# Linear attention and a mixture of experts: each row of x carries its gate as a fifth piece of 128 words

## The chip, the cores and the metric

The kernel runs on one core of a Trainium2 chip. The metric is the device time of one execution in microseconds; lower is better. The engines have separate, in-order instruction streams and meet by semaphores: TensorE (PE in the profile, with its weight loads as PEld), VectorE (DVE), ScalarE (ACT), GpSimd (POOL) and SyncE (SP), which here only issues DMAs.

## What is computed

Two stages, the second on the result of the first:

```python
# attention, per batch b and head h: q, k, v (8, 8, 576, 64), w_phi (64, 128)
proj = x @ w_phi;  proj -= max(abs(proj), -1)
phi(x) = concat([exp(proj), exp(-proj)], -1)
attn = (phi(q) @ (phi(k).T @ v)) / (phi(q) @ sum_s phi(k) + 1e-6)
x = attn.transpose(0, 2, 1, 3).reshape(4608, 512)
# experts: w_gate (512, 8), w1 (8, 512, 1024), w2 (8, 1024, 512)
logits = x @ w_gate
expert = argmax(logits);  gate = softmax(logits)[expert]
out[t] = gate[t] * (relu(x[t] @ w1[expert[t]]) @ w2[expert[t]])
```

Every row goes through one expert only.

## The kernel before, in words

**Attention.** 16 units (4 groups of 4 pairs of heads) are worked off one after another, up to about 385 us. SP loads `xr` (q and k, line 235) and `vt` (v, lines 345 and 358). A hand-written plan (`PLAN_...`, `plan_of`) says at which step of a unit which load, split and product is issued; an entry "C" calls `constants2()` in unit 2. The finished rows of x go to `x_dram` in HBM by `store_rows` (lines 217 and 222), a table of 4608 rows of 512 words. The routing of a group works out each row's expert and gate; `gate_store` writes the gate (four equal words a row) by the same helper to a second table, `g_dram`, of 4608 x 4 words.

**Blocks.** The rows of one expert are put together into blocks of 128. Two blocks of an expert make a pair. There are 19 pairs (u = 0 to 18, blocks 0 to 37) and then single blocks (u = 19, 20, 21: blocks 38, 39, 40; more lie in a conditional part, which is not taken here). `gidx` holds for each block the numbers of its rows in x, `sidx` those in the output. Blocks 0 to 2, the lead, are put together from the first three groups while the last one is still in attention.

**Fetching a block.** GpSimd gathers rows by indirect DMA (`fetch_rows`, line 861), in one of two ways:

- `gather_rows`: one DMA, 128 rows of 512 words, into the tile `xg`. Used for u < 4 and for the single blocks. `x_parts` then turns the block with four TensorE transposes against `ident` (line 1104).
- `gather_quarters`: four DMAs of 128 rows of 128 words. The indices `qidx` are such that partition p gets quarter rows of 32-row groups, so that one VectorE instruction that turns 32 x 32 squares (line 1099) turns the whole block. Used where `by_quarters(u)` holds: 4 <= u < 19.

Either way ScalarE casts the turned block `px` into a high part `xh` (line 1105), and VectorE takes the rest `xl` (line 1106). All products of float32 numbers are made of such high and low parts, three matmuls each. `xg` has four buffers, so a gather waits until the block four places earlier has been turned.

**Gates.** `gather_gates` fetches a block's 128 gates from `g_dram` by one more indirect DMA into a tile `gate` (six buffers), issued by `gates(u)` beside `gather(u + 1)`.

**Expert stage.** For a pair, `pair_first` makes `pm` (lines 1123 to 1125), ScalarE makes `hh` (line 1130) and VectorE `hl` (line 1131), and `pair_second` adds up `po` (lines 1143 to 1145), a quarter of the 1024 hidden words at a time; `first_product`, `h_parts` and `second_product` do the same for a single block. `write` scales `po` by the gate on ScalarE into `ob` (line 1191, three buffers) and sends it out by an indirect DMA (line 1193), which waits for the write before it. SP loads the weights `raw`, ScalarE casts them to `wh` (line 1057), VectorE, and GpSimd for a few, take the rest `wl` (line 1058).

The order of instructions on each engine is worked out by the framework's scheduler from the program (`behind(a, b)` makes it put a after b); GpSimd's and SP's DMAs each use eight semaphores in turn (DMASW and DMAHW in the rows below).

## Time and profile before

| | before |
|---|---|
| median of 3 runs | 885.82 us (885.74 to 887.44) |
| the profiled execution | 887.59 us, span 885.9 us |
| granted TensorE clock, mean | 0.991 |
| indirect gathers of row quarters (x120) | 153.4 us, 1279 ns each |
| indirect gathers of gates (x41) | 50.3 us, 1228 ns each |
| indirect gathers of whole rows (x11) | 11.4 us, 1036 ns each |
| indirect writes of the output (x41) | 47.7 us, 1163 ns each |
| VectorE turns (x30) | 33.0 us, 1102 ns each |
| TensorE transposes of x (x44) | 7.5 us, 288 ns each |

A row of a timeline has the start in us, the duration, the engine, the line of the kernel, the operation, the tile written and those read, and in brackets how long the engine stood idle before it and what released it ("issue": nothing that the profile shows). Groups give the count, the busy time and the mean in ns. Consecutive instructions of one kind are put together as xN. A matmul's end is modelled and overlaps the next, so that TensorE's pace is the distance of starts.

### The profile page before, as it was taken

How to read it: one execution, taken by the hardware profiler on the slowest of the kernel's cores; microseconds unless marked ns; L12 is line 12 of the kernel's file. 1: busy time of each engine (PE TensorE's matmuls, PEld its weight loads, DVE VectorE, ACT ScalarE, POOL GpSimd, SP SyncE). 2: the span in 40 equal slices, each digit the busy share in tenths (PEclk: the TensorE clock that was granted, in tenths of full speed). 3: DMA queues.
4: the chain of work that ended last, by engine and by line, in shares of the span. 5: the costliest groups of instructions: out<-in, count | busy, mean ns of one | idle time of the engine just before them, and what ended most of it. 6: DMA issues, size and time to landing. Idle time of an engine off the chain costs nothing. (4 is left out here: it accounts for less than half of the span.)

```text
span 885.9 us, 18042 instructions
## 1 busy us (share of the span) xinstructions
PE 866.7 (98%) x6617; PEld 812.4 (92%) x6617; DVE 620.0 (70%) x1041; ACT 571.7 (65%) x874; POOL 547.1 (62%) x398
## 2 busy tenths in 40 slices
PE   9999999999999999999899999999999999999996
PEld 6999999999999999998688999998999989999884
DVE  6678878878887788759487666666766667765441
ACT  5888888888888888553465555555555555555662
POOL 5677667776676668553667888746876466312331
PEclk9999999999999999999899999999999999999998
DMA  6233334333343333351253154531545544445540
GB/s 203 84 98 98 107 112 95 82 95 104 111 113 110 111 111 71 108 185 20 82 162 112 55 171 125 173 110 49 160 126 164 184 160 142 135 142 188 200 141 15
DMA packets 69548, 106.65 MB, mean 120 GB/s; under 512 B 13582, under 2 KB 31502, under 8 KB 69456
## 3 DMA queue, kind: packets, MB, share of 16 engines
q1 hardware_dynamic: 59312, 84.50, 31.8%
q0 software_dynamic: 9472, 20.81, 7.6%
q8 instruction: 53, 0.87, 0.4%
q14 instruction: 39, 0.32, 0.1%
q10 hardware_dynamic: 672, 0.15, 0.1%
HBM read 128.42 MB, written 20.26 MB: 168 GB/s over the span
## 5 line engine op out<-in xcount | busy, mean ns | idle before, releaser
L1058 DVE TENSOR_TENSOR wl<-raw,wh 128x1024 fp32r<-128x1024 f32 x160 | 196.1, 1235 | 111.6 <-ACT wh L1057 79.7
L1057 ACT CAST wh<-raw 128x1024 fp32r<-128x1024 f32 x168 | 174.9, 1048 | 94.9 <-PE po L1145 41.5
L861 POOL DMA_INDIRECT xg<-x_dram,qidx x120 | 153.4, 1279 | 76.2 <-DVE px L1099 37.1
L448 PE MATMUL pn<-kf,qp 128*128 128x73 f32 (+1 forms) x1152 | 185.5, 256 | 0.0
L313 POOL TENSOR_TENSOR kl<-e,kh 128x1024 fp32r<-128x1024 f32 x45 | 107.5, 2388 | 106.7 <-ACT kh L311 99.1
L448 PEld LDWEIGHTS pn<-kf,qp 128*128 128x128 f32 x1152 | 172.5, 190 | 0.5
L1125 PE MATMUL pm<-xh,wl 128*128 128x256 f32 x608 | 172.4, 284 | 0.5 <-issue 0.5
L1124 PE MATMUL pm<-xl,wh 128*128 128x256 f32 x608 | 172.6, 284 | 0.1
L1123 PE MATMUL pm<-xh,wh 128*128 128x256 f32 x608 | 171.9, 283 | 0.0
L285 DVE TENSOR_REDUCE mx<-ps_proj 128x4 f32<-128x512 f32 (+1 forms) x160 | 101.0, 633 | 59.6 <-PE ps_proj L281 56.9
L1143 PE MATMUL po<-wh,hh 128*128 128x512 f32 x304 | 120.8, 398 | 3.9 <-issue 3.9
L1144 PE MATMUL po<-wl,hh 128*128 128x512 f32 x304 | 120.2, 395 | 0.6 <-issue 0.6
L1124 PEld LDWEIGHTS pm<-xl,wh 128*128 128x128 f32 x608 | 116.6, 192 | 3.7 <-issue 0.8
L1123 PEld LDWEIGHTS pm<-xh,wh 128*128 128x128 f32 x608 | 116.7, 192 | 2.9
L1145 PE MATMUL po<-wh,hl 128*128 128x512 f32 x304 | 119.2, 393 | 0.0
L1125 PEld LDWEIGHTS pm<-xh,wl 128*128 128x128 f32 x608 | 116.5, 192 | 0.8 <-issue 0.7
L286 DVE TENSOR_TENSOR t<-ps_proj,mx 128x512 f32<-128x512 f32 (+1 forms) x160 | 101.4, 635 | 4.9
L378 PE MATMUL pk<-kh,vl 128*64 128x256 f32 x300 | 101.6, 339 | 0.0
L378 PE MATMUL pk<-kh,vh 128*65 128x256 f32 x300 | 99.5, 332 | 1.5 <-ACT kvT L410 1.5
L378 PE MATMUL pk<-kl,vh 128*65 128x256 f32 x300 | 100.3, 334 | 0.0
L245 POOL TENSOR_TENSOR xl<-xr,xh 128x640 fp32r<-128x640 f32 (+1 forms) x60 | 96.8, 1633 | 2.1 <-ACT xh L244 2.1
L1130 ACT ACTIVATE hh<-pm 128x512 fp32r<-128x512 f32 x76 | 45.4, 597 | 76.4 <-PE pm L1125 56.4
(217 smaller groups left out, 1902.9 us busy)
## 6 DMA issues: line engine op xcount, KB each, us to landing
raw<-w SPq DMA_DIRECT2D x168, 512.0 KB
vt<-vv SPq DMA_DIRECT2D x15, 640.0 KB
x_dram<-xrow SPq DMA_DIRECT2D x30, 256.0 KB
xr<-kT SPq DMA_DIRECT2D x15, 320.0 KB
xr<-qT SPq DMA_DIRECT2D x15, 320.0 KB
xr<-kT SPq DMA_DIRECT2D x17, 256.0 KB
xr<-qT SPq DMA_DIRECT2D x17, 256.0 KB
xg<-x_dram,qidx POOLq DMA_INDIRECT x120
```

The costliest lines, as they stand in the source:

```text
L313: eng.tensor_tensor(kl, e[:, 0:m], kh, op=ALU.subtract)
L378: return T.matmul(st["pk", bb][0:n, hh, :], (vl if j == 1 else vh)[:, 2 * (c + (bb if c == 8 else 0)) + hh, 0:n], (kl if j == 2 else kh)[: ...
L448: m = T.matmul(pn[:, i - a, :] if c < 8 else pn[:, 2 + hh : 6 : 2, :], qp[:, s, s0 + hh, :], st["kf"][:, hh, s, c // 4, :] if c < 8 else s ...
L861: return G.indirect_dma_start(out=out, out_offset=None, in_=source[0:rows], in_offset=bass.IndirectOffsetOnAxis(ap=index, axis=0), bounds_ ...
L1057: A.copy(th, raw[k])
L1058: m = (G if k in (POOL_LO0 if u == 0 else POOL_LO if u >= NPAIR else ()) else V).tensor_tensor(tl, raw[k], th, op=ALU.subtract)
L1123: T.matmul(pm[:, i], th, xh[:, k, :], start=(k == 0), stop=False)
L1124: T.matmul(pm[:, i], th, xl[:, k, :], start=False, stop=False)
L1125: T.matmul(pm[:, i], tl, xh[:, k, :], start=False, stop=(k == KD - 1))
L1143: T.matmul(po, hh[:, i, r], th[:, c], start=(i == j == 0), stop=False)
L1144: T.matmul(po, hh[:, i, r], tl[:, c], start=False, stop=False)
L1145: T.matmul(po, hl[:, i, r], th[:, c], start=False, stop=(i == 1 and j == 3))
```

## The change

1. `x_dram` gets rows of 640 words: 512 of x, four with the gate (columns 512 to 515, written by `store_rows` as before to `g_dram`), and 124 zeros. The zeros come from a new tile `nought` (one GpSimd memset in `constants2`) and are written by four SP DMAs of 128 x 9 x 124 words, one for each group, in units 2 to 5 of the plan's "C".
2. `g_dram`, `gather_gates`, `gates` and their 41 DMAs are gone. `xg` has five pieces of 128 words. A gather of whole rows brings the gate with it; `gather_quarters` fetches a fifth piece, whose indices (a fifth column of `qidx`, one more VectorE operation) are those of the rows in their plain order. `x_parts` ends with a VectorE copy of one word per row, `gate <- xg[:, 4, 0:1]`.
3. `by_quarters(u)` holds for all u >= 4: the single blocks too come in pieces and are turned by VectorE. Row gathers go from 11 to 8, pieces from 120 to 165, VectorE turns from 30 to 33, TensorE transposes of x from 44 to 32.
4. `spread` and the two halves of `eg` use buffers of the pool `op`.

```diff
-    x_dram = dram.tile([NT, DM], F32, name="x_dram")
-    g_dram = dram.tile([NT, XW], F32, name="g_dram")
+    x_dram = dram.tile([NT, XQ * P], F32, name="x_dram")
...
             elif what == "C":
                 if st["u"] == 2:
                     constants2()
+                if 2 <= st["u"] < 2 + NG:
+                    g = st["u"] - 2
+                    rows = x_dram[g * NC * P : (g + 1) * NC * P, DM + XW :]
+                    nc.sync.dma_start(
+                        rows.rearrange("(c p) w -> p c w", p=P), nought.unsqueeze(1).to_broadcast([P, NC, P - XW])
+                    )
...
-            store_rows(g, gt, g_dram, 0, XW, c0, n)
+            store_rows(g, gt, x_dram, DM, XW, c0, n)
...
-        xg = xgp.tile([P, 4, P], F32, name="xg")
-        quarters = x_dram.rearrange("t (q d) -> (t q) d", q=4)
-        for c in range(4):
-            behind(fetch_rows(xg[:, c, :], quarters, qidx[:, c, b : b + 1], 4 * NT), st["experts"])
+        xg = xgp.tile([P, XQ, P], F32, name="xg")
+        for c in range(XQ):
+            behind(fetch_rows(xg[:, c, :], parts_dram, qidx[:, c, b : b + 1], XQ * NT), st["experts"])
         return xg
 
-    def gather_gates(b, after):
-        gate = xgp.tile([P, XW], F32, name="gate", bufs=6)
-        index, rows = (gidx0, NEARLY * P) if b < NLEAD else (gidx, NT)
-        behind(fetch_rows(gate, g_dram, index[:, b : b + 1], rows), after)
-        return gate
+    parts_dram = x_dram.rearrange("t (q d) -> (t q) d", q=XQ)
...
-        spread = raw2.tile([P, 4, P], F32, name="spread")
+        spread = op.tile([P, 4, P], F32, name="spread", tag="ob", bufs=3)
...
-        V.tensor_scalar(qidx, pq, 4.0, quad, op0=ALU.mult, op1=ALU.add)
+        V.tensor_scalar(qidx[:, 0:4], pq, float(XQ), quad, op0=ALU.mult, op1=ALU.add)
+        V.tensor_scalar(qidx[:, 4], st["rows"], float(XQ), 4.0, op0=ALU.mult, op1=ALU.add)
...
     def by_quarters(u):
-        return 4 <= u < NPAIR
+        return u >= 4
...
-            V.transpose(px, xg.rearrange("p c (d k) -> p c k d", k=KD))
+            V.transpose(px, xg[:, 0:4].rearrange("p c (d k) -> p c k d", k=KD))
...
         V.tensor_tensor(xl, px, xh, op=ALU.subtract)
+        gate = xgp.tile([P, 1], F32, name="gate", bufs=6)
+        V.tensor_copy(gate, xg[:, 4, 0:1])
+        st["gate", blocks(u)[i]] = gate
```

In the order of the instructions, the change shows at these three places. (Rows give the line, the operation, the tiles with their numbers and the semaphores that the instruction waits for; the change's lines are a few higher or lower than those of before.)

VectorE, at the end of pair u = 1 and in pair u = 2 (the profile's 456 to 467 us). Before, behind the last `hl` of u = 1:

```order
L1131 SCALAR_TENSOR_TENSOR hl_6699<-pm_6673,hh_6698 128x512 [waits Activation_49]
L1058 TENSOR_TENSOR wl_6944<-raw6_5828,wh_6943 128x1024 [waits DMAHW5_49,PE_49,Activation_49]
L1058 TENSOR_TENSOR wl_6872<-raw0_5816,wh_6871 128x1024 [waits DMAHW2_49,PE_49,Activation_49]
L1131 SCALAR_TENSOR_TENSOR hl_6794<-pm_6768,hh_6793 128x512 [waits Activation_49]
L1058 TENSOR_TENSOR wl_6939<-raw1_5818,wh_6938 128x1024 [waits DMAHW4_49,Activation_49]
L1058 TENSOR_TENSOR wl_7039<-raw7_5830,wh_7038 128x1024 [waits DMAHW7_49,Activation_49]
```

And now (`xg_6719` and `xg_6735` are blocks 8 and 9, which pair u = 4 will use):

```order
L1133 SCALAR_TENSOR_TENSOR hl_6694<-pm_6668,hh_6693 128x512 [waits Activation_49]
L1107 COPY gate_7126<-xg_6719 128x1 [waits DMASW0_49,Activation_49]
L1107 COPY gate_7192<-xg_6735 128x1 [waits DMASW5_49,Activation_49]
L1063 TENSOR_TENSOR wl_6941<-raw6_5833,wh_6940 128x1024 [waits DMAHW1_49,PE_49,Activation_49]
L1063 TENSOR_TENSOR wl_6867<-raw0_5821,wh_6866 128x1024 [waits DMAHW6_49,PE_49,Activation_49]
L1133 SCALAR_TENSOR_TENSOR hl_6787<-pm_6761,hh_6786 128x512 [waits Activation_49]
```

Two copies stand between that `hl` and the next weight splits. They wait for the fifth pieces of blocks 8 and 9 (DMASW0, DMASW5) and for ScalarE to be done with the `gate` buffers.

GpSimd, at the same place. Before, the second block's pieces, the two writes with the next gates, and the next pieces:

```order
L861 DMA xg_6737<-x_dram_155,qidx_71 128x128 [waits DMASW3_49]
L1193 DMA out<-ob_6714,sidx0_74 4608x512 [waits DMASW4_49,Activation_49]
L861 DMA gate_7025<-g_dram_156,gidx_68 128x4 [waits DMASW5_49]
L861 DMA gate_7029<-g_dram_156,gidx_68 128x4 [waits DMASW6_49,Activation_49]
L1193 DMA out<-ob_6719,sidx_69 4608x512 [waits DMASW7_49,DMASW4_49]
L861 DMA xg_6999<-x_dram_155,qidx_71 128x128 [waits DMASW0_49,PE_49]
L861 DMA xg_6999<-x_dram_155,qidx_71 128x128 [waits DMASW1_49]
```

And now:

```order
L870 DMA xg_6735<-x_dram_156,qidx_71 128x128 [waits DMASW4_49]
L870 DMA xg_6735<-x_dram_156,qidx_71 128x128 [waits DMASW5_49]
L1195 DMA out<-ob_6709,sidx0_74 4608x512 [waits DMASW6_49,Activation_49]
L1195 DMA out<-ob_6714,sidx_69 4608x512 [waits DMASW7_49,DMASW6_49,Activation_49]
L870 DMA xg_6996<-x_dram_156,qidx_71 128x128 [waits DMASW0_49,DVE_49,PE_49]
L870 DMA xg_6996<-x_dram_156,qidx_71 128x128 [waits DMASW1_49]
```

The two gates between the writes are gone, and the fifth piece of block 9 stands ahead of the first write. The second write waits for the first (DMASW6) as it did before (DMASW4).

SP, in the early attention units. Before:

```order
L235 DMA xr_516<-kT 128x640 [waits DMAHW4_49,DMAHW0_49,Pool_49]
L235 DMA xr_575<-qT 128x640 [waits DMAHW5_49,Pool_49]
L235 DMA xr_638<-kT 128x512 [waits DMAHW7_49,Pool_49]
L345 DMA vt_697<-vv 128x1280 [waits DMAHW6_49,DMAHW3_49]
L235 DMA xr_719<-qT 128x512 [waits DMAHW0_49,Pool_49]
```

And now:

```order
L238 DMA xr_516<-kT 128x640 [waits DMAHW4_49,DMAHW0_49,Pool_49]
L238 DMA xr_575<-qT 128x640 [waits DMAHW5_49,Pool_49]
L598 DMA x_dram_156<-nought_147 128x9x124
L598 DMA x_dram_156<-nought_147 128x9x124 [waits DMAHW3_49]
L598 DMA x_dram_156<-nought_147 128x9x124 x2
L238 DMA xr_638<-kT 128x512 [waits DMAHW7_49,DMAHW6_49,Pool_49]
L348 DMA vt_697<-vv 128x1280
L238 DMA xr_719<-qT 128x512 [waits DMAHW0_49,Pool_49]
```

The four stores of zeros, which the program issues in four units, stand together between a load of q and the next load of k.

More of the change, by code (lines that the diff above doesn't have):

```diff
@@ L49 @@
 XW = 4
+XQ = 5
 Q = P // 4
@@ L81, in tile_linear_attention_moe @@
     eidx = keep.tile([1, NB], I32, name="eidx")
-    qidx = keep.tile([P, 4, NB], I32, name="qidx")
+    qidx = keep.tile([P, XQ, NB], I32, name="qidx")
     nblk = keep.tile([1, 1], I32, name="nblk")
@@ L139, in constants @@
         nc.scalar.dma_start(fold[0:D, :, D + 1 : W], w_gate.rearrange("(h d) e -> d h e", d=D))
+    nought = const.tile([P, P - XW], F32, name="nought")
     def constants2():
+        G.memset(nought, 0.0)
         G.memset(ltri, 1.0)
@@ L877, in gather_quarters @@
     def gather_quarters(b):
-        xg = xgp.tile([P, 4, P], F32, name="xg")
-        quarters = x_dram.rearrange("t (q d) -> (t q) d", q=4)
-        for c in range(4):
-            behind(fetch_rows(xg[:, c, :], quarters, qidx[:, c, b : b + 1], 4 * NT), st["experts"])
-        return xg
-    def gather_gates(b, after):
-        gate = xgp.tile([P, XW], F32, name="gate", bufs=6)
-        index, rows = (gidx0, NEARLY * P) if b < NLEAD else (gidx, NT)
-        behind(fetch_rows(gate, g_dram, index[:, b : b + 1], rows), after)
-        return gate
+        xg = xgp.tile([P, XQ, P], F32, name="xg")
+        for c in range(XQ):
+            behind(fetch_rows(xg[:, c, :], parts_dram, qidx[:, c, b : b + 1], XQ * NT), st["experts"])
+        return xg
+    parts_dram = x_dram.rearrange("t (q d) -> (t q) d", q=XQ)
     v_tiles = []
@@ L1008, in experts_of @@
         V.tensor_reduce(nblk, ends[:, 1], axis=AX.X, op=ALU.max)
-        eg = sg.tile([1, 2, NB, E], F32, name="eg")
+        eg = [op.tile([1, NB, E], F32, name="eg", tag="h") for _ in range(2)]
         places = ((first[0:1], ends[:, 0], 0, 2 * NPAIR), (start[0:1], ends[:, 1], 2 * NPAIR, NB))
@@ L1013, in experts_of @@
                 m = V.tensor_tensor(
-                    eg[:, j, n0:n1],
+                    eg[j][:, n0:n1],
                     iota_p[0:1, n0:n1].unsqueeze(2).to_broadcast([1, n1 - n0, E]),
@@ L1019, in experts_of @@
                 behind(m, st["places"])
-        G.tensor_tensor(eg[:, 0], eg[:, 0], eg[:, 1], op=ALU.subtract)
-        st["experts"] = G.tensor_tensor(eg[:, 0], eg[:, 0], iota_e[0:1].unsqueeze(1).to_broadcast([1, NB, E]), op=ALU.mult)
+        G.tensor_tensor(eg[0], eg[0], eg[1], op=ALU.subtract)
+        st["experts"] = G.tensor_tensor(eg[0], eg[0], iota_e[0:1].unsqueeze(1).to_broadcast([1, NB, E]), op=ALU.mult)
         with nc.allow_low_precision("experts are integers"):
-            V.tensor_reduce(eidx, eg[:, 0], axis=AX.X, op=ALU.add)
+            V.tensor_reduce(eidx, eg[0], axis=AX.X, op=ALU.add)
     st = {}
@@ L1080, in gather @@
                     st["xg", b] = gather_rows(gidx[:, b : b + 1], NT, st.get("experts"))
-    def gates(u):
-        if u < lim[0]:
-            for b in blocks(u):
-                if ("gate", b) not in st:
-                    st["gate", b] = gather_gates(b, st["experts"])
     def x_parts(u, i):
@@ L1219, in tile_linear_attention_moe @@
     go(nums[-8:])
-    st["low"] = weights(0, 3)
-    for b in range(NLEAD):
-        st["gate", b] = gather_gates(b, st["low"])
+    weights(0, 3)
     run(r1[1:3])
@@ L1252, in tile_linear_attention_moe @@
     quarters_of()
-    gates(1)
     gather(2)
@@ L1277, in tile_linear_attention_moe @@
                 gather(u + 2)
-                gates(u + 1)
             for du, k in AHEAD_W[j]:
@@ L1293, in step @@
     def step(u):
-        gates(u)
         gather(u + 3)
```

## The prediction

> **What bounds the kernel now.** I read the busy times first, then a table of windows, then the list of what each engine waited for, and last the timelines at the places that the change touches. From the page:
>
> ```profile
> span 885.9 us, 18042 instructions
> PE 866.7 (98%) x6617; PEld 812.4 (92%) x6617; DVE 620.0 (70%) x1041; ACT 571.7 (65%) x874; POOL 547.1 (62%) x398
> ```
>
> TensorE is busy for 866.7 of 885.9 us, so 19.2 us are idle. The windows (length, busy time of each engine with its instructions, granted clock, DMA share, GB/s) say where:
>
> ```profile
> 0.00:22.00 22.00, 20.17 (x94) 15.01 (x95) 15.29 (x35) 12.71 (x25) 11.56 (x41) 1.00 0.66 204
> 420.00:440.00 20.00, 15.64 (x82) 13.19 (x82) 7.42 (x13) 7.72 (x11) 13.89 (x13) 0.83 0.32 94
> 440.00:520.00 80.00, 79.86 (x514) 72.60 (x514) 58.90 (x62) 48.31 (x61) 58.70 (x46) 1.00 0.37 113
> 780.00:860.00 80.00, 79.96 (x475) 71.04 (x474) 41.88 (x44) 45.60 (x59) 22.39 (x15) 1.00 0.52 172
> 860.00:886.00 26.00, 17.51 (x85) 14.08 (x83) 4.82 (x6) 6.44 (x10) 5.97 (x4) 0.89 0.09 33
> ```
>
> In the expert part TensorE has no gap (79.86 of 80, 79.96 of 80). There a matmul that goes saves its own length, and a wait on VectorE or GpSimd costs only what it makes TensorE wait. The gaps are at the two ends and at 420 to 440, where 4.4 us are lost (20 - 15.64) and the clock is 0.83. That last gap is one wait; first TensorE's matmul behind it, then the ScalarE activation that it needed:
>
> ```profile
> 434.05 0.79 PE L1143 MATMUL po<-wh,hh 128*128 128x512 f32 x1 [3.90 <-issue]
> 433.39 0.60 ACT L1130 ACTIVATE hh<-pm 128x512 fp32r<-128x512 f32 x1 [6.05 <-remote]
> ```
>
> The activation stood 6.05 us after its matmuls could be done, and its releaser ("remote") is nothing that the profile shows.
>
> **The change, part by part.**
>
> 1. TensorE loses 12 transposes. The three single blocks (u = 19, 20, 21) are now turned by VectorE, so three groups of four go. Their rows, with the next instruction on TensorE:
>
> ```profile
> 828.94 0.65 PE L1104 MATMUL px<-ident,xg 128*128 128x128 f32 x4
> 829.35 0.48 PE L1143 MATMUL po<-wh,hh 128*128 128x512 f32 x1
> 845.97 0.63 PE L1104 MATMUL px<-ident,xg 128*128 128x128 f32 x4
> 846.44 0.82 PE L1170 MATMUL pht<-ident,h 128*128 128x128 f32 x6
> 847.30 0.19 PEld L1157 LDWEIGHTS pm<-wh,xh 128*128 128x128 f32 x1 [0.27 <-ACT xh L1105]
> 853.11 0.64 PE L1104 MATMUL px<-ident,xg 128*128 128x128 f32 x4
> 853.51 0.48 PE L1183 MATMUL po<-wh,hh 128*128 128x512 f32 x1
> ```
>
> The groups take 829.35 - 828.94 = 0.41, 0.47 and 0.40 us of TensorE's time, 1.28 in all. The matmul after two of them is drawn out, 0.48 instead of the usual 0.39 to 0.40, about 0.08 each. The second group is followed by a wait of 0.27 for the cast of its own result, which goes too, since that block is now turned a pair earlier. Sum 1.28 + 0.16 + 0.27 = 1.7; I take **-1.6** (from -1.3, the groups alone, to -1.7). TensorE stands behind no other engine there, so nothing else is late next.
>
> 2. GpSimd and VectorE in the pairs. The groups, with busy us and mean ns:
>
> ```profile
> L861 POOL DMA_INDIRECT xg<-x_dram,qidx x120 | 153.4, 1279 | 76.2 <-DVE px L1099 37.1
> L861 POOL DMA_INDIRECT gate<-g_dram,gidx x41 | 50.3, 1228 | 12.3 <-issue 11.7 <-ACT wh L1057 0.3 <-ACT xh L1105 0.3
> L628 DVE TENSOR_SCALAR spare<-spare 128x1 f32<-128x1 f32 x1 | 0.1, 147 | 0.0
> ```
>
> 41 gate gathers go. 33 blocks (30 of pairs, 3 single) now take five pieces: 165 instead of 120, and three row gathers go. That is 45 - 41 - 3 = +1 instruction: GpSimd's load is the same, twelve DMAs in a pair (8 + 2 + 2 before, 10 + 2 now), at 1.3 + 0.3 us each some 19 of the 22.5 us that a pair takes (from TensorE's row at 490.62, below, to the same row of the next pair at 513.10). What differs is the order. A gate used to come after the eight pieces and the write; now the fifth piece stands ahead of the write, and the output of a pair is sent later. VectorE gains three turns of 1.1 us (482.06, below), under pairs in which it is idle a quarter of the time, and 41 copies of one word per row. No row shows such a copy; it lies between nothing and the 1.1 us of a turn, and I take the 0.15 us of the operation on one word per row (L628): 41 x 0.15 = 6 us beside 620, hidden under TensorE at either end (41 x 1.1 = 45 of the 266 us in which VectorE is idle).
>
> The copies' price is where they stand. VectorE runs in order, and the order shows the copies of two blocks ahead of two splits (wl) and of the hl that TensorE needs. First for blocks 8 and 9:
>
> ```profile
> 446.57 1.94 POOL L861 DMA_INDIRECT xg<-x_dram,qidx  x1 [0.30 <-issue]
> 456.81 1.00 POOL L861 DMA_INDIRECT xg<-x_dram,qidx  x1 [0.30 <-issue]
> 446.41 4.62 DVE L1058 TENSOR_TENSOR wl<-raw,wh 128x1024 fp32r<-128x1024 f32 x4
> 459.75 1.23 DVE L1058 TENSOR_TENSOR wl<-raw,wh 128x1024 fp32r<-128x1024 f32 x1 [3.08 <-ACT wh L1057]
> 462.36 0.68 DVE L1131 SCALAR_TENSOR_TENSOR hl<-pm,hh 128x512 fp32r<-128x512 f32 x1
> 467.35 0.40 PE L1145 MATMUL po<-wh,hl 128*128 128x512 f32 x1
> 418.63 1.04 POOL L861 DMA_INDIRECT xg<-x_dram,gidx  x1 [5.97 <-DVE emp L980]
> 422.10 0.75 PE L1104 MATMUL px<-ident,xg 128*128 128x128 f32 x4 [0.46 <-DMA xg<-x_dram,gidx]
> ```
>
> Before, the eighth piece ended at 457.81. Two more at 1.0 + 0.3 (VectorE has no split there) end at 460.4. A gather lands 422.10 - 419.67 = 2.4 us after GpSimd's end, so the copies pass at 462.8, and hl, which ended 459.75 -> 463.04 = 3.3 us after the first split began, ends at 466.1. TensorE reads it at 467.35: stall **0**. With two drawn-out pieces (2 x 2.24) and the slowest landing that I find (6.6, below) the copies pass at 468.9 and hl ends at 472.2: stall 4.9.
>
> The Trainium skill ("GPSIMD Engine Reference", section "Key points") says that GpSimd shares its SBUF interfaces with VectorE and is held up by VectorE instructions with two SBUF inputs. The trace agrees: a piece takes 1.94 us beside the four wl splits at 446.41 and 1.00 when VectorE stands. By that rule the pieces can't be drawn out while VectorE waits for them, which leaves only the landing for the upper end.
>
> Second, blocks 10 and 11, whose pieces stand behind block 3's write, and that behind block 2's:
>
> ```profile
> 458.38 1.02 POOL L1193 DMA_INDIRECT out<-ob,sidx  x1 [0.57 <-ACT ob L1191]
> 465.98 1.02 POOL L1193 DMA_INDIRECT out<-ob,sidx  x1 [3.92 <-DMA out<-ob,sidx]
> 478.31 1.42 POOL L861 DMA_INDIRECT xg<-x_dram,qidx  x1 [0.31 <-issue]
> 482.06 1.13 DVE L1099 STREAM_TRANSPOSE px<-xg 128x512 f32<-128x512 f32 x1
> 483.57 1.23 DVE L1058 TENSOR_TENSOR wl<-raw,wh 128x1024 fp32r<-128x1024 f32 x1 [0.38 <-ACT wh L1057]
> 486.13 0.68 DVE L1131 SCALAR_TENSOR_TENSOR hl<-pm,hh 128x512 fp32r<-128x512 f32 x1
> 490.62 0.39 PE L1145 MATMUL po<-wh,hl 128*128 128x512 f32 x1
> 513.10 0.39 PE L1145 MATMUL po<-wh,hl 128*128 128x512 f32 x1
> ```
>
> A write held the next one until 465.98 - 459.40 = 6.6 us after its own end. Block 2's write now ends at 461.7, block 3's starts at 468.3, and ten pieces from 469.6 at 1.28 + 0.30 end at 485.4. They land at 487.7 (before: 479.73 to 482.06, 2.3 us). hl began 486.13 - 483.57 = 2.56 us after the first split and takes 0.68, so it ends at 491.0 against 490.62: stall **0.4**. With all pieces at 1.9 it would be 3 more.
>
> The Trainium skill ("DMA: Bandwidth & Descriptors", section "Anatomy of one DMA") gives some 2.0 us of fixed completion time for a small DMA. For the gathers the trace agrees (2.3 and 2.4 us); for the writes it doesn't (6.6). By the page block 3's write would start at 463.7 and there would be no stall here: the sum would be 0.4 us lower.
>
> One pair later the lag is under 3 us and GpSimd, with 19 of 22.5 us, has caught up by the fifth pair. I take **+0.4** for all pairs, from 0 to +5.
>
> 3. Zeros. SP now issues four stores of zeros (128 x 9 x 124 words each, 2.29 MB) between the two loads below (ahead of them GpSimd's nearest memset, behind them ScalarE's cast of the second load):
>
> ```profile
> 0.94 0.59 POOL L136 MEMSET fold<- 65x584 f32 x1
> 18.27 0.33 SPq L235 DMA_DIRECT2D xr<-qT  x1
> 32.39 0.33 SPq L235 DMA_DIRECT2D xr<-kT  x1
> 38.78 0.62 ACT L244 CAST xh<-xr 128x512 fp32r<-128x512 f32 x1 [1.46 <-PE ps_proj L280]
> ```
>
> The window 0 to 22 moved 204 GB/s at a share of 0.66, 309 at a full share; 2.29 MB then take 7.4 us and are over by 27, in a stretch where SP's queue had nothing. I take **0**. At half that rate (pieces of 496 bytes) they end near 34, and at a third near 41; then the load of 32.39 lands at 36 or 43 against its cast at 38.78, and TensorE, which follows the cast, would wait 0 to 4 us; I put the end at 2, since half the rate is the nearer. On GpSimd one memset of 124 words per row goes into the constants; one of 584 words took 0.59, so 0 to 0.6 us, taken as 0, since the loads that GpSimd waits for at the start set the pace there. The gate stores keep their number and size.
>
> 4. Lead and transition. Three of the 41 gate gathers go from the lead part. At the transition the copies of blocks 3, 4 and 5 stand ahead of two splits; block 5's gather takes the place of this row,
>
> ```profile
> 424.63 1.00 POOL L861 DMA_INDIRECT xg<-x_dram,gidx  x1 [0.30 <-issue]
> ```
>
> ends at 425.6 and lands at 428.0, so hl can begin at 428.0 + 2.6 = 430.6 and end at 431.3. TensorE waited until 434.05 for another reason, so this is hidden: **0**. If that reason goes, TensorE waits for hl instead (rival 1).
>
> **Sum**: -1.6 + 0.4 = -1.2. The profiled execution took 887.59 with a span of 885.9; its run lies 1.8 above the median of 885.82. I carry the difference over to the median: 885.8 - 1.2 = **884.6 us**, -0.14%. That is inside 0.2% (1.8 us), about what a measurement of this kernel can tell from no change.
>
> **Rivals.**
> - *The gap at 430 closes.* For it: its releaser isn't in the profile, GpSimd's list of DMAs beside it changes (two gates fewer before 434), and so what holds it may move. Against it: ScalarE's order there is the same. TensorE would go on at 431.3 instead of 434.05 at the latest for hl: 884.6 - 2.75 = 881.9; with the lower clock of that window gone too (0.17 of 15.64 us, 2.7), 879.2.
> - *The fifth piece holds VectorE, VectorE holds TensorE* (the slower side). Place: copies of blocks 8 to 11. It decides when the fifth piece lands more than 3.6 us after GpSimd's end at block 9 (467.35 - 3.3 - 460.4), or when pieces take over 1.3 us on the mean at block 11. Half of the upper ends, 2.5 + 1.7 = 4.2 us instead of 0.4: 884.6 + 3.8 = 888.4. For it: wl splits draw pieces out to 1.9. Against it: gathers land in 2.4.
> - *The zeros delay the early loads*: +2, 886.6; with the memset's 0.3 and the 0.4 of the pairs drawn out, up to 888.
> - *The transposes go but their time does not*: the singles then wait for the splits of weights instead. 79.96 busy of 80 speaks against it. 885.8 + 0.4 = 886.2.
>
> **How the numbers follow.** Forecast 0.40, of which 0.12 lies below 884.05 (faster by 0.2%) since -1.2 is 0.6 from that bound. The gap closes: 0.26, all faster. The fifth piece: 0.20, of which 0.18 is above 887.6. Zeros: 0.08, slower. Time not saved: 0.06, same. Faster 0.38, same 0.28 + 0.02 + 0.06 = 0.36, slower 0.26. The range reaches over rival 1's 881.9 with two thirds of its clock term (880.0) and over rival 2's 888.4 with half as much stall again on the first place (889.0). The forecast's own range is 883.7 to 886.0.
>
> **What would show it.** Right: no L1104-like rows on TensorE behind 475, TensorE's busy time lower by about 1.4; the copies of blocks 8 to 11 show idle VectorE of 3 us and more, and the hl matmuls after them under 0.5; the next load of k after the zeros at 32 to 33. Wrong: an idle TensorE of over 1 us between 460 and 515 (second rival), before 60 (third), or a gap at 430 that has moved by over 1 us (first). Outside these places TensorE's rows should be the same; a shift elsewhere, above all at the end, where the last write began 2.5 us after its data, would be a thing that I haven't seen.

## The result and the profile after

| | before | after |
|---|---|---|
| median | 885.79 us (885.74 to 887.44, 4 runs) | 894.76 us (893.45 to 896.17, 4 runs) |
| ratio | | 1.0095 (95% interval 1.0079 to 1.0112) |
| profiled execution | 887.59 us, span 885.9 | 894.73 us, span 893.0 |

The change makes the kernel about 1% slower. The forecast was 884.6 us with a range from 880.0 to 889.0; the time lies 5.8 us above the range.

The page of after, busy time of each engine:

```profile
PE 870.2 (97%) x6605; PEld 811.9 (91%) x6605; DVE 627.4 (70%) x1086; ACT 570.3 (64%) x874; POOL 541.9 (61%) x400
```

Windows of after at the same places as before (22 to 50 is where the zeros are stored):

```profile
22.00:50.00 28.00, 28.00 (x246) 26.86 (x245) 20.47 (x39) 24.53 (x43) 17.57 (x9) 1.00 0.56 153
420.00:440.00 20.00, 18.52 (x120) 16.32 (x119) 15.35 (x22) 13.96 (x18) 10.72 (x10) 1.00 0.35 110
440.00:520.00 80.00, 70.57 (x400) 60.26 (x399) 45.37 (x56) 35.64 (x47) 54.69 (x47) 0.91 0.33 102
```

Two things have changed. The gap between 420 and 440 has shrunk (15.64 busy at a clock of 0.83 before, 18.52 at 1.00 now), and a window that was full, 440 to 520, now has 9.4 us of idle TensorE, 114 matmul rows fewer than the 514 of before, and a clock of 0.91.

**A ledger.** The scaling of a finished block on ScalarE (`ob`) happens 41 times in both kernels and marks how far the work is. Blocks 0, 4, 6, 34, 38 and 40 in the timeline of before:

```profile
423.58 1.38 ACT L1191 ACTIVATE ob<-po,gate 128x512 f32<-128x512 f32 x2
481.18 1.42 ACT L1191 ACTIVATE ob<-po,gate 128x512 f32<-128x512 f32 x2 [0.67 <-DMA xg<-x_dram,qidx]
503.66 1.42 ACT L1191 ACTIVATE ob<-po,gate 128x512 f32<-128x512 f32 x2 [1.41 <-PE po L1145]
819.97 1.42 ACT L1191 ACTIVATE ob<-po,gate 128x512 f32<-128x512 f32 x2 [1.47 <-PE po L1145]
859.25 0.69 ACT L1191 ACTIVATE ob<-po,gate 128x512 f32<-128x512 f32 x1 [0.31 <-PE po L1185]
877.55 0.69 ACT L1191 ACTIVATE ob<-po,gate 128x512 f32<-128x512 f32 x1 [4.75 <-PE po L1185]
```

and the same blocks in that of after:

```profile
422.98 1.37 ACT L1193 ACTIVATE ob<-po,gate 128x512 f32<-128x512 f32 x2
475.58 1.42 ACT L1193 ACTIVATE ob<-po,gate 128x512 f32<-128x512 f32 x2 [0.88 <-PE po L1147]
514.36 0.69 ACT L1193 ACTIVATE ob<-po,gate 128x512 f32<-128x512 f32 x1 [2.82 <-PE po L1147]
831.26 1.42 ACT L1193 ACTIVATE ob<-po,gate 128x512 f32<-128x512 f32 x2 [1.47 <-PE po L1147]
868.80 0.69 ACT L1193 ACTIVATE ob<-po,gate 128x512 f32<-128x512 f32 x1 [0.31 <-PE po L1187]
887.10 0.69 ACT L1193 ACTIVATE ob<-po,gate 128x512 f32<-128x512 f32 x1 [4.75 <-PE po L1187]
```

After minus before, block by block: -0.60, -5.60, +10.70, +11.29, +9.55, +9.55. So the changed kernel is ahead by 5.6 us at block 4, loses 16.3 us between blocks 4 and 6, moves little for 300 us, and wins 1.74 at the single blocks.

The rest is at the very end. The last two writes on GpSimd in the timeline of before:

```profile
873.08 1.00 POOL L1193 DMA_INDIRECT out<-ob,sidx  x1 [2.13 <-ACT ob L1191]
880.80 0.98 POOL L1193 DMA_INDIRECT out<-ob,sidx  x1 [6.73 <-issue]
```

and in that of after:

```profile
884.10 0.99 POOL L1195 DMA_INDIRECT out<-ob,sidx  x1 [3.57 <-issue]
888.07 0.98 POOL L1195 DMA_INDIRECT out<-ob,sidx  x1 [2.97 <-ACT ob L1193]
```

Before, the last write began 2.56 us after its data were there (877.55 + 0.69 to 880.80); after, 0.28. With the rest of the tail (5.1 and 4.9 us from that write to the end of the span) this is -2.4 us. Sum: 9.55 - 2.4 = +7.1, which is the difference of the spans.

**Where the 16.3 us are lost.** Slices of 10 us in after:

```profile
480.00:490.00 10.00, 7.71 (x43) 6.00 (x42) 4.95 (x5) 1.82 (x2) 7.87 (x8) 1.00 0.18 47
490.00:500.00 10.00, 8.24 (x43) 6.02 (x43) 1.92 (x2) 1.65 (x2) 7.87 (x8) 1.00 0.23 67
500.00:510.00 10.00, 5.72 (x21) 4.19 (x21) 3.74 (x4) 3.55 (x5) 6.69 (x7) 0.60 0.22 66
510.00:520.00 10.00, 10.00 (x46) 8.55 (x46) 7.08 (x10) 6.14 (x8) 3.76 (x4) 0.72 0.10 33
```

Every engine but GpSimd (POOL) does far less than before: TensorE starts 43, 43 and 21 matmuls in the first three slices, where the full window of before has 64 in 10 us (514 in 80). What that looks like in the timeline of TensorE's weight loads:

```profile
507.71 0.29 PEld L1127 LDWEIGHTS pm<-xh,wl 128*128 128x128 f32 x1 [0.91 <-issue]
508.45 0.29 PEld L1125 LDWEIGHTS pm<-xh,wh 128*128 128x128 f32 x1 [0.46 <-issue]
509.18 0.29 PEld L1126 LDWEIGHTS pm<-xl,wh 128*128 128x128 f32 x1 [0.44 <-issue]
509.90 0.29 PEld L1127 LDWEIGHTS pm<-xh,wl 128*128 128x128 f32 x1 [0.43 <-issue]
```

and on ScalarE:

```profile
487.65 1.04 ACT L1062 CAST wh<-raw 128x1024 fp32r<-128x1024 f32 x1 [6.88 <-remote]
502.74 1.04 ACT L1062 CAST wh<-raw 128x1024 fp32r<-128x1024 f32 x1 [6.10 <-remote]
```

TensorE's loads come one every 0.72 us here instead of one every 0.12 to 0.23, and they wait for nothing that the profile shows. Between 485 and 490 SyncE goes at the same beat, in register operations that wait for no one: they start at 486.91, 487.60, 488.30, 489.01 and 489.71, TensorE's loads beside them at 486.95, 487.64, 488.35 and 489.74. "Remote" is what ScalarE was put down to in the gap at 430 before. GpSimd's rows in that stretch (the first, one in the middle, the last):

```profile
461.98 1.88 POOL L870 DMA_INDIRECT xg<-x_dram,qidx  x1 [0.99 <-PE px L1103]
...
474.23 1.00 POOL L870 DMA_INDIRECT xg<-x_dram,qidx  x1 [0.30 <-issue]
...
507.52 1.00 POOL L870 DMA_INDIRECT xg<-x_dram,qidx  x1 [0.30 <-issue]
```

GpSimd issues 32 indirect DMAs from 461.98 to 508.5 without a pause longer than its usual 0.3 us, 24 of them at its quickest pace of 1.0 us. TensorE's slow loads, or ticks, begin at 485 and end at 510.2, 1.7 us after the series; from 490.7 to 494 its loads come at their usual pace.

### The profile page after: what moved, and what is told of

It reads as the page before. It is cut to its first block, busy times and chain, and to the rows that moved or that the text cites. A ratio compares the mean times of both kernels' runs of the same rounds, so it can differ in the third digit from the quotient of the medians.

```text
span 893.0 us, 18079 instructions
## 1 busy us (share of the span) xinstructions
PE 870.2 (97%) x6605; PEld 811.9 (91%) x6605; DVE 627.4 (70%) x1086; ACT 570.3 (64%) x874; POOL 541.9 (61%) x400
## 5 line engine op out<-in xcount | busy, mean ns | idle before, releaser
L870 POOL DMA_INDIRECT xg<-x_dram,qidx x165 | 200.1, 1213 | 64.3 <-issue 45.7
L1195 POOL DMA_INDIRECT out<-ob,sidx x41 | 47.8, 1165 | 105.4 <-ACT ob L1193 84.8
```

The costliest lines, as they stand in the source:

```text
L870: return G.indirect_dma_start(out=out, out_offset=None, in_=source[0:rows], in_offset=bass.IndirectOffsetOnAxis(ap=index, axis=0), bounds_ ...
```

## The experiments

Two theories. **S**: a long series of GpSimd's indirect DMAs without a pause and at full pace holds up the instruction streams of all other engines until it ends; the change joins the series of several pairs into one, since the gates no longer stand between the writes and a write waited only 2.5 us for the one before it. (The kernel before has a long series too, 60 DMAs from 473.6 to 569.4, but with at most three quick ones in a row; so the pace is part of the theory.) **V**: the copies of the gates, which VectorE makes ahead of two splits and of `hl`, hold VectorE, and VectorE holds TensorE. The kernel before ran beside each, on the same chip. It took 877.4 and 877.7 us on two of the four chips used for these runs and 885.0 to 885.8 on the other two, so times are compared on one chip only. Of the two where it takes 877 us (the first chip and the last), neither ran the changed kernel as it is.

### First chip (before 877.74 us)

Pacing: one GpSimd addition of 128 x 256 behind every second piece of blocks 8 to 15.

```diff
+            m = fetch_rows(xg[:, c, :], parts_dram, qidx[:, c, b : b + 1], XQ * NT)
+            behind(m, st["experts"])
+            if 8 <= b < 16:
...
+                if "pause" in st:
+                    behind(m, st["pause"])
+                if c % 2:
+                    st["pause"] = G.tensor_tensor(pad, pad, pad, op=ALU.add)
+                    behind(st["pause"], m)
```

> The change, with one GpSimd addition of 128x256 behind every second piece of blocks 8 to 15 (its result is used by nothing); the gate copies stay where the change puts them. In the trace of the change TensorE was idle 9.4 us between 440 and 520 and had a clock of 0.60 and 0.72 from 500 to 520, just while GpSimd sent ten and more DMAs at its fast pace (1.0 us each, 0.3 between) without a break. Theory S (the unbroken series of DMAs holds up the other engines): no series above 6, the stall is gone, 878 to 883 us. Theory V (the copies hold VectorE, and it holds TensorE): nothing changes, 893 to 896 us.

Late copies: `xg` is released later, so that GpSimd's next gather waits, and VectorE's order is changed too.

```diff
-        V.tensor_copy(gate, xg[:, 4, 0:1])
+        m = V.tensor_copy(gate, xg[:, 4, 0:1])
+        if "hl" in st:
+            behind(m, st["hl"])
```

> The change, with each gate copy ordered behind the hl that was made last before it in the program, so that no copy of a later pair stands ahead of the splits and the hl of this one. Theory V: 878 to 883 us, the stall at 485 to 510 gone. Theory S: by the longest unbroken fast series in the trace; where it is 9 or more, a stall stands at its end and the time is 888 to 895 us; where VectorE, no longer held, draws the pieces out by its splits and the series stays under 8, there is no stall and 878 to 883 us.

The kernel before with such an addition behind each of the 11 gathers from 423 us on:

> The kernel before, with one GpSimd addition of 128x256 behind each of the eleven gathers that begin at 423 us (its result is used by nothing). There the trace of before has a series of nine fast DMAs and TensorE's gap of 3.9 us at 430 with a clock of 0.50 behind it. Theory S: the gap and the low clock go, about 4.1 + 2.4 us: 878 to 881 us. Theory V says nothing of before: no change, 885 to 887 us. If the gap is one of the transition itself (weights, the value of the expert): no change either.

and with eight more gathers of gates (128 x 4 words, read by nothing) behind those of pair 3:

```diff
+            if u == 2:
+                more = op.tile([P, 8, XW], F32, name="more", bufs=1)
+                for n in range(8):
+                    behind(fetch_rows(more[:, n, :], g_dram, gidx[:, 4:5], NT), st["gated"])
```

> The kernel before, with eight more gathers of 128 gates (16 bytes a row, into a tile that nothing reads) behind the gates of pair 2, so that GpSimd's series at 423 us is eight DMAs longer, some 10 us. Theory S: the stall at 430 lasts as long as the series, to 445 and more, 6 to 14 us more: 891 to 900 us. Theory V and a cause in the transition: 885 to 887 us, since the added gathers are read by nothing; blocks 8 and 9, fetched behind them, come up to 6 us later, with 8 us of slack before they are turned.

| | median us | ratio to before (95%) |
|---|---|---|
| paced, blocks 8 to 15 | 878.05 | 1.0007 (0.9993 to 1.0020) |
| late copies | 875.58 | 0.9973 (0.9962 to 0.9983) |
| before, 11 gathers paced | 879.47 | 1.0024 (1.0013 to 1.0036) |
| before, eight more gathers | 885.12 | 1.0082 (1.0058 to 1.0105) |

Neither edit of the changed kernel shows a stall. But the kernel before is 8 us quicker here than on the chip of the result, so this says little of the stall itself. Eight gathers of 2 KB cost the kernel before 7.4 us, and TensorE has a gap of 4.3 us at 482, not at 445, where S had it. That gap is an ordinary wait: the next pieces came later, VectorE stood in front of its turn, and `hl` was late.

```profile
480.34 1.09 DVE L1104 STREAM_TRANSPOSE px<-xg 128x512 f32<-128x512 f32 x1 [8.05 <-DMA xg<-x_dram,qidx]
482.06 0.80 PE L1150 MATMUL po<-wh,hl 128*128 128x512 f32 x1 [4.28 <-DVE hl L1136]
```

GpSimd's series there is the longest of all, 107 DMAs from 423 to 590 with up to 11 quick ones in a row, and TensorE shows no tick in it. On this chip, then, such a series doesn't stall the engines; S can hold only where the kernel before takes 885 us.

### Second and third group (before 885.78 and 885.35 us)

Both kernels once more, and the parts of the change apart. Only the single blocks by quarters and VectorE, on the kernel before:

```diff
     def by_quarters(u):
-        return 4 <= u < NPAIR
+        return u >= 4
```

and the reverse, the whole change without that line.

> The changed kernel as it is, beside runs of before in the same job. The kernel before took 885.8 us when the change was timed and 877.7 us beside the four experiments so far, so its stall at 430 us comes and goes. If the change's stall at 485 to 510 belongs to its order of instructions, it is there again: 893 to 896 us. If it comes and goes like that of before, the change without it takes 894.7 less 9.4 us of idle TensorE and some 6 us of low clock: 877 to 881 us.

> The kernel before as it is, for its trace in the same job. If 877.7 us is the time without the stall, TensorE's gap of 3.9 us at 430 and the clock of 0.50 behind it are not in this trace, and the rest of it is as before: 876 to 879 us with a span of 875 to 877. If something else made it faster, the gap is still there.

> The kernel before with one line of the change: the single blocks too come by quarter rows and are turned by VectorE; gates from their table as before. TensorE loses 12 transposes, my term of -1.6 us (from -1.3 to -1.7). Against before in the same job: 1.6 us less, ratio 0.998, if the stalls are alike in both; the transposes at 829, 846 and 853 us gone in the trace.

> The change without that line: the single blocks gathered whole and turned by TensorE, all else as in the change. Against the change in the same job 1.6 us more, if the stalls are alike; its order of instructions up to pair 16 is that of the change, so a stall that belongs to the order is the same in both.

| | median us (range) | ratio to before (95%) |
|---|---|---|
| after again | 903.54 (877.76 to 911.08, 4 runs) | none given: one run stands far below the others |
| before again | 885.7 | |
| only the single blocks | 883.57 (880.16 to 890.91) | 0.9991 (0.9955 to 1.0027) |
| all but the single blocks | 916.9 (914.12 to 918.06) | 1.0337 (1.0311 to 1.0362) |

The loss is not fixed. One of the four runs of after came out at 877.76, as if the stall weren't there, and the others at 901 to 911. In the profiled one the stall is in the same place, 482 to 508, and so it is without the single blocks' part. That part is therefore not the cause. (Some 7.7 us of the 916.9 belong to the program's end; see the last section.) Alone, its time isn't told from no change. The kernel before has its gap at 430 again in its trace (3.9 us).

Then the first chip's edits where the stall shows:

> The changed kernel once more, now in one job with the three kernels that took the stall away on another chip. Where before takes 885.8 us in this job (its stall at 430 is there): 894 to 911 us with the stall at 482 to 508. Where before takes 877.7 (no stall): 877 to 880 us.

> The change with GpSimd's series for blocks 8 to 15 broken by additions, the copies where they were, beside the change itself. Theory S: no stall in either state of the chip, 876 to 880 us. Theory V: as the change in this job, 894 us and more where before takes 885.8.

> The change with the copies behind the hl, beside the change itself. Both theories 874 to 878 us; under S only because VectorE's splits break the series, whose longest fast part was 3 to 5 up to 520 us in the trace of the first time.

> The kernel before with GpSimd's series at 423 us broken, beside before. Where before has its stall at 430 (885.8 us): theory S 878 to 881 us, ratio 0.992 to 0.995; any cause other than the series: no change. Where before has no stall (877.7): 879 to 880 us, as the first time.

| | median us | ratio to before (95%) |
|---|---|---|
| after, third time | 895.82 | 1.0121 (1.0076 to 1.0165) |
| paced, blocks 8 to 15 | 894.11 | 1.0101 (1.0063 to 1.0139) |
| late copies | 877.61 | 0.9908 (0.9873 to 0.9943) |
| before, 11 gathers paced | 892.53 | 1.0063 (1.0029 to 1.0096) |

By S the paced kernels should have lost the stall. Their time didn't, and the profile says why. Windows of the changed kernel, paced:

```profile
480.00:520.00 40.00, 39.28 (x251) 35.47 (x250) 30.56 (x34) 20.52 (x27) 34.94 (x29) 1.00 0.34 104
520.00:560.00 40.00, 31.90 (x141) 24.68 (x140) 14.62 (x17) 11.60 (x16) 26.63 (x25) 0.75 0.34 107
```

and of the kernel before, paced:

```profile
420.00:440.00 20.00, 19.54 (x128) 17.51 (x128) 16.88 (x22) 15.32 (x19) 17.26 (x16) 1.00 0.31 89
480.00:520.00 40.00, 31.03 (x164) 26.13 (x163) 21.14 (x22) 13.65 (x17) 27.88 (x23) 0.83 0.18 56
```

In both the stall has left the paced stretch (480 to 520 in the one, 420 to 440 in the other) and stands in the next unpaced one: 25 DMAs from 520 to 554 in the first, 36 from 454 to 508 in the second. That the gap at 430 in the kernel before goes in this way speaks for its being of the same kind. Late copies beat both kernels, but they take away the series and move the copies at once, so S and V both allow it.

### The deciding pair (before 884.99 us)

The copies where they were and no long series at all: the addition behind the third piece of every block from 8 on.

```diff
-            if 8 <= b < 16:
+            if 8 <= b < 2 * NPAIR + 3:
...
-                if c % 2:
+                if c == 2:
```

> The changed kernel with one GpSimd addition of 128x256 behind the third fifth-row piece of every block from 8 on: no series of indirect DMAs runs on unbroken for more than some seven. S (a long unbroken fast series holds up the sequencers of all engines until it ends): neither the stall at 482 to 510 nor that at 532 to 554 of the partly paced kernel is there, time 876 to 881 on a chip where the kernel before takes 885. V (the hoisted copies of the gates on VectorE hold back hl, and so TensorE): the copies stand where they stood, time 893 or more.

The copies late, and a long series put back: small gathers behind the writes of blocks 4 to 15.

```diff
+        if "filled" in st:
+            behind(m, st["filled"])
+        if 4 <= b < 16:
...
+            for n in range(3 if b % 2 else 2):
+                k = 5 * (b // 2 - 2) + (2 + n if b % 2 else n)
+                d = fetch_rows(st["more"][:, k, :], words_dram, qidx[:, 4, b : b + 1], XQ * NT)
+                behind(d, st.get("filled", m))
+                behind(d, m)
+                st["filled"] = d
```

> The changed kernel with its gate copy behind the last hl, and between blocks 4 and 15 two or three small gathers of 128x4 words behind each write on GpSimd (30 in all, read by nothing), which fill the pauses in which its queue waits for xg. VectorE's and TensorE's instructions stay in the order of the quick kernel with late copies. S: an unbroken series of 20 or more DMAs is there again between 440 and 560, and with it TensorE in ticks of 0.7 us until the series ends; 885 or more where the kernel with late copies takes 877. V: 877 to 879, for the copies are late.

> The changed kernel with its gate copy ordered behind the last hl, a third time, as the base for its companions here: 876 to 879 by both theories.

Late copies, with the single blocks by TensorE again:

> The same with the single blocks turned by TensorE as in the kernel before: the twelve transposes are the one difference, and no long series is in either. If the transposes are worth what their busy time says, 1.3 to 1.7 us more than the kernel with late copies (878 to 880); if TensorE has them free beside its waits, no more than 0.5.

| | median us | ratio to before (95%) |
|---|---|---|
| paced, all blocks | 873.80 | 0.9881 (0.9861 to 0.9902) |
| late copies, pauses filled | 903.91 | 1.0213 (1.0190 to 1.0235) |
| late copies | 877.16 | 0.9910 (0.9894 to 0.9927) |
| late copies, single blocks by TensorE | 886.46 | 1.0015 (1.0005 to 1.0025) |

The window from 480 to 520 of the kernel paced in all blocks:

```profile
480.00:520.00 40.00, 40.00 (x260) 36.57 (x260) 28.98 (x33) 20.84 (x27) 33.81 (x27) 1.00 0.37 113
```

and of the one with the pauses filled:

```profile
480.00:520.00 40.00, 35.56 (x215) 29.87 (x214) 25.60 (x31) 18.61 (x24) 29.14 (x26) 1.00 0.25 72
```

V is right in neither. With the copies early and GpSimd's series cut to seven at most, TensorE is full, and the kernel, with 33 additions that nobody needs, is 1.2% faster than before. The traces have VectorE's, ScalarE's and TensorE's instructions in the same order as in after; VectorE even stood 5.27 us in front of a copy at 456, against 3.68 in after, and TensorE went on. So it is GpSimd's queue that made the difference, as S has it. The changed kernel as it is didn't run beside this one; that the stall belongs to this chip too is taken from the kernel before (884.99) and from the next kernel.

With the copies late and the pauses filled, again with the other engines' order unchanged, 30 gathers of 2 KB cost 26.8 us (2.4 of them at the end, see the last section). The ticks are back, as S has it: between 546 and 550 loads come at 546.59, 547.32, 548.02, 548.75 and 549.46 behind nothing, such as

```profile
548.02 0.19 PEld L1130 LDWEIGHTS pm<-xh,wl 128*128 128x128 f32 x1 [0.52 <-issue]
```

But the price is not the stall's alone. Of TensorE's long waits between 461 and 642 us (those of the table below, 22 us in all) the profile puts some 10 down to nothing and some 11 to `hl`, which was late because the pieces were:

```profile
532.95 1.13 DVE L1099 STREAM_TRANSPOSE px<-xg 128x512 f32<-128x512 f32 x1 [3.69 <-DMA xg<-x_dram,qidx]
536.97 0.19 PEld L1150 LDWEIGHTS po<-wh,hl 128*128 128x128 f32 x1 [2.18 <-DVE hl L1136]
```

GpSimd had 17 DMAs a pair to send instead of 12; 34 of them took 49.9 us from 499.7 on, so 17 take some 25, more than the 22.5 of a pair. This is plain overload, which S doesn't need. A pause of the late copies in GpSimd's timeline (of their run before this one):

```profile
482.03 1.00 POOL L1197 DMA_INDIRECT out<-ob,sidx  x1 [2.54 <-ACT hh L1134]
485.61 1.04 POOL L870 DMA_INDIRECT xg<-x_dram,qidx  x1 [2.58 <-DVE gate L1107]
```

and what stands there in the filled kernel:

```profile
484.22 1.25 POOL L1198 DMA_INDIRECT out<-ob,sidx  x1 [0.30 <-issue]
485.78 1.03 POOL L870 DMA_INDIRECT more<-x_dram,qidx  x1 [0.30 <-issue]
```

How long is too long? From the timelines, a series being DMAs with pauses up to 0.45 us, quick ones those of up to 1.15 us, and the loss the sum of TensorE's distances between weight loads that are over 0.45 us, less 0.24 each (in brackets what the profile puts down to a late `hl`, where that is over 0.5):

| kernel, from-to us | DMAs | most quick ones in a row | loss us |
|---|---|---|---|
| before, 424-439 | 11 | 9 | 4.4 |
| after, 462-509 | 32 | 10 | 12.5 |
| after again, 460-506 | 32 | 11 | 16.7 |
| paced in blocks 8 to 15, 520-554 | 25 | 8 | 13.4 |
| before paced, 454-508 | 36 | 8 | 13.0 (2.7) |
| pauses filled, 462-496 | 23 | 7 | 5.6 (1.4) |
| pauses filled, 500-550 | 34 | 8 | 8.1 (3.1) |
| pauses filled, 553-596 | 29 | 9 | 5.6 (4.1) |
| pauses filled, 599-640 | 28 | 7 | 2.6 (2.6) |
| after, 565-580 | 11 | 8 | 0.7 |
| late copies, 462-479 | 12 | 5 | 0 |
| before, 474-570 | 60 | 3 | 0.3 |
| paced in all blocks, any behind 440 | up to 7 | up to 6 | 0 |
| first chip: before, eight more gathers, 423-590 | 107 | 11 | 4.7 (4.7) |
| first chip: paced in blocks 8 to 15, 521-654 | 85 | 6 | 0 |

Length alone doesn't do it (60 DMAs, of them at most three quick ones in a row), and eight quick ones with a pause behind them cost little. On the chips where it appears, the stall goes with a quick series that goes on; but two such series of the filled kernel (553 to 640) lose little or nothing to it, so the table gives no bound. On the first chip the same partly paced kernel has an even longer series at the same place, and no stall. Part of it is a circle, which the table can't take apart: a piece is drawn out to some 2 us beside VectorE's splits, and a VectorE that is stopped makes none.

The last two kernels of the group lie 9.3 us apart, instead of the 1.3 to 1.7 expected of the twelve transposes. TensorE's work ends only 1.83 us later (871.27 against 869.44). The other 7.6 us lie behind the last write, where TensorE has nothing to do: see the last section.

### Both paced (before 877.42 us)

> The kernel before, with one GpSimd addition of 128x256 behind every fourth gather from 423 us on, to the end. If long fast series are all that the kernel before loses at 430 us, its gap of 4.3 us goes and does not come back later as it did when only the first 11 gathers were paced: 876 to 881. If pacing helps for a reason that belongs to the changed kernel alone, 885 or more. The change itself, with neither kernel disturbed, is then worth the distance to the paced changed kernel: 1.3 to 1.7 us by the transposes' busy time, 1.8 by the end of TensorE's work in the last pair of kernels.

> The changed kernel paced in every block, again, as the companion of the paced kernel before on the same chip: 873 to 877.

The kernel before paced behind every fourth gather took 880.44 us, ratio 1.0034 (1.0021 to 1.0047), and the changed one paced in all blocks 874.5, ratio 0.9972 (0.9958 to 0.9987). This chip again was one on which the kernel before takes 877, so what was to be settled, whether pacing alone brings it down from 885, stays open. In its place the run shows that pacing has a price: the additions put the writes off, and ScalarE then waited for a buffer of `ob`, with TensorE 2 us behind it:

```profile
526.30 0.69 ACT L1203 ACTIVATE ob<-po,gate 128x512 f32<-128x512 f32 x1 [7.38 <-DMA out<-ob,sidx]
529.42 0.50 PE L1155 MATMUL po<-wh,hh 128*128 128x512 f32 x1 [2.05 <-ACT hh L1142]
```

The kernel paced in all blocks has the lowest ratio to before of all kernels run (0.9881), and is below it on both chips on which it ran; late copies come to the same on a chip where before takes 877 (0.9973).

## Why the prediction was wrong, step by step

- **Part 2 failed, and there the sentence "GpSimd's load is the same ... What differs is the order".** It priced the order only by when a fifth piece reaches VectorE. What the order did was to let GpSimd run the pieces of several pairs in one series at full pace; the stall in it cost 16.3 us between blocks 4 and 6, where the sum had +0.4 and at the most +5. (Of the 16.3, 12.5 are TensorE's long waits; the clock of 0.60 and 0.72 from 500 to 520 would fit the rest.) Its own mechanism didn't come about. The copies of blocks 8 and 9 waited for ScalarE to be done with the `gate` buffers, not for the pieces, and those of 10 and 11 hardly at all. VectorE's rows:

```profile
456.20 0.15 DVE L1107 COPY gate<-xg 128x1 f32<-128x1 f32 x1 [3.68 <-ACT ob L1193]
456.78 0.15 DVE L1107 COPY gate<-xg 128x1 f32<-128x1 f32 x1 [0.42 <-ACT ob L1193]
479.50 0.15 DVE L1107 COPY gate<-xg 128x1 f32<-128x1 f32 x1 [0.18 <-issue]
```

  and the writes of blocks 2 and 3 on GpSimd:

```profile
456.45 1.02 POOL L1195 DMA_INDIRECT out<-ob,sidx  x1 [2.20 <-ACT ob L1193]
459.99 1.00 POOL L1195 DMA_INDIRECT out<-ob,sidx  x1 [2.52 <-ACT hh L1132]
```

  The copies passed at 456.9 and 479.7 (forecast 462.8 and 487.7). The second write went 2.5 us after the first, not 6.6. By the row of before, block 3's write would have started at 468.3 and GpSimd would have paused; it started at 459.99, and the series followed. Before, GpSimd runs 60 DMAs on after that pause, so the missing pause alone doesn't explain the loss; why the pieces run at 1.00 us here, where before VectorE's splits draw them out, wasn't taken apart. The duration taken for a copy, 0.15 us, is right.
- **The place to look was named and read as another case.** The prediction said of a stop of TensorE between 460 and 515 that it would speak for the second rival. It came there, by another mechanism. The rival's price, 4.2 us, was not its size either. Its sum was short besides: ten pieces at 1.9 us instead of 1.28 are 6.2 us later, not 3, which puts the rival at 890.0 (half of 4.9 and half of 6.6 are 5.8 in place of 0.4), still 4.8 under the measured time. In the same way, half as much again on the first place's 2.5 adds 1.2 to the range's upper end, not 0.6.
- **Rival 1 happened**, beside the loss, and drew the time the other way. The gap at 430 went and TensorE waited for `hl` instead, as the rival had it (forecast 431.3):

```profile
428.66 0.60 ACT L1132 ACTIVATE hh<-pm 128x512 fp32r<-128x512 f32 x1 [2.44 <-remote]
431.00 0.50 PE L1147 MATMUL po<-wh,hl 128*128 128x512 f32 x1 [0.72 <-DVE hl L1133]
```

  It was worth 5.0 us by the ledger from block 0 to block 4, against 2.75 to 5.4. The reason can now be read: before, 11 DMAs ran without a pause from 423.3 to 438.4; without the gates they are five, and then come pauses:

```profile
427.65 1.01 POOL L870 DMA_INDIRECT xg<-x_dram,gidx  x1 [0.30 <-issue]
430.32 1.01 POOL L1195 DMA_INDIRECT out<-ob,sidx  x1 [1.67 <-ACT wh L1062]
436.98 1.15 POOL L870 DMA_INDIRECT xg<-x_dram,qidx  x1 [5.64 <-PE px L1103]
```

  A gap "whose releaser isn't in the profile" was in the page of before, next to the longest quick series of that trace. Reading it as a cost of that series, and asking where the change makes such a series longer, might have led to the loss. (The 6.05 us read there as a delay of the activation are ScalarE's idle time; the last matmul into `pm` ended at 430.15, 3.2 us before it.)
- **Part 1 was right.** The forecast was -1.6 (from -1.3 to -1.7); the ledger has -1.74 between blocks 34 and 38, and the kernels with the transposes on TensorE show 0.0 to +0.24 there. The kernel before with the single blocks' line alone shows -1.79. Of the rivals, "their time doesn't go" falls by this.
- **Part 3 was right.** The window from 22 to 50 is full (28.00 of 28) at a DMA share of 0.56 instead of 0.25, and the load of k is issued at 32.44, against 32.39 before. The rival of the zeros falls.
- **Part 4** is right as far as the copies go, and gave rival 1 its time.
- **The end** was named as a thing that hadn't been seen: it gave -2.4 us, which isn't in the sum.

With the stall left out, the ledger gives -0.6 - 5.0 + 0.6 - 1.74 - 2.4 = -9.1 us. Late copies ran 7.8 us under before on that chip and pacing 11.2 us under, so a kernel without the stall lies about there. By that sum the time without the stall would be near 876.7, under the stated range (from 880.0) as well: the forecast's sum also lacked rival 1 and the end.

## What to carry to other kernels

Where one engine issues DMAs back to back, its pauses are part of the schedule: before taking an instruction or a wait out of such a queue, count how many DMAs then run on without a pause and at what pace, and look in the trace for what the quickest such series already costs the other engines. A stop that the profile puts down to nothing, at the same time on several engines, is a sign of a shared cause and should be looked for in what the one busy engine is doing. Taking the wait away can then be dearer than the wait; on chips where the kernel before takes 885 us the change lost 1% against it, and with a useless addition every fifth DMA it won 1.2%.

## What the runs showed of the hardware

- **Engines slowed down together, waiting for no one.** For much of GpSimd's series TensorE's weight loads came every 0.70 to 0.72 us, and SyncE's register operations in the same ticks, while VectorE and ScalarE stood for up to 6.9 us. GpSimd's queue wasn't full: the packets of a gather began some 0.7 us after the end of its DMA instruction and took some 0.5 us (those of the last, which ended at 508.52, came from 509.22 to 509.73), and were through before the next one's began. The Trainium skill ("Trainium Architecture — The Big Picture", section "What this means for kernel authors") calls the engines independent and, on the engines' side of SBUF, names VectorE's and GpSimd's shared port pair alone as contended. The trace differs: TensorE, which has no part in that pair, lost 12.5 us. That the series sets it off, on the chips where it appears, is shown by pacing, and the ticks of the filled kernel bear it out. What in the chip does it wasn't found; why the runs on two chips show none of it, and one run in four of the changed kernel on another none either, stays open. Every run on record has a span and a clock from the chip's own records, so none shows whether making those records has a part in it.
- **The end of the program depends on the number of GpSimd's DMAs.** The trace has a DRAIN on GpSimd behind the last write. It takes 0.73 us with 213 indirect DMAs in the program, 0.81 with 214, 1.39 with 221, 1.47 with 222 and 3.26 with 244, that is 0.08 us a DMA. But with 202 (the two kernels with the fifth piece and the single blocks by TensorE) it takes 8.49. That is 7.7 us of the 9.3 by which the last of the deciding group was slower, and both kernels that undo only that part of the change pay it.
- **A write of the output doesn't always hold the next for 6.6 us.** In the kernel before and its paced forms the last write began 6.73 to 6.99 us after the end of the one ahead of it, with its data there. In after it began 2.97 us after it, and waited for its data, so the hold was no longer than that; the write at 459.99 began 2.52 us after the one at 456.45. The Trainium skill ("DMA: Bandwidth & Descriptors", section "Anatomy of one DMA") gives some 2.0 us of fixed time for a small DMA, and here the trace comes near it. What makes the long ones wasn't tried.
